# A split-product attention and MoE kernel on one core: the second chunk in whole float32 products with its softmax sums from ones beside the values, and each weight conversion issued behind a named ScalarE instruction

## The chip, the cores and the metric

The kernel runs on one core of one Trainium2 chip. The metric is device time in microseconds of one execution, taken as the median of several; lower is better. The core has TensorE (PE, matrix products), VectorE (DVE), ScalarE (ACT), GpSimd (POOL) and SyncE (SP, which issues the transfers here). In the profile PEld is TensorE loading the operand that stays in place, and a line number such as L460 is the line of the kernel as listed below.

## The reference, cut to what matters

```python
def _attn_ref(q, k, v, n_sink, window):          # B, H, S, D = 4, 8, 768, 64; n_sink, window = 4, 128
    scores = scale * np.matmul(q, k.transpose(0, 1, 3, 2))
    keep = is_sink | in_window                   # the first n_sink keys, and the last `window` keys up to the query
    scores = np.where(keep, scores, -1000000000.0)
    scores = scores - np.max(scores, axis=-1, keepdims=True)
    a = np.exp(scores)
    a = a / (np.sum(a, axis=-1, keepdims=True) + 1e-09)
    return np.matmul(a, v)

def _moe_ref(x, w_in, w_out, s, b):              # x: 3072 x 512, w_in: 512 x 2048, w_out: 2048 x 512
    h = x @ w_in
    r = np.maximum(h, 0.0)
    g = s * (r * r) + b
    return g @ w_out
```

The heads' outputs, put side by side, are the rows of `x`. All inputs and the result are float32.

## The kernel before, in words

The 3072 rows are cut into eight chunks of 384 queries: chunk c is half c % 2 of batch c // 2. For each chunk there is an attention part, which produces `x` (transposed: 512 features in four blocks `cc` of 128 partitions, 384 columns), and an MoE part over 16 blocks f of 128 of the 2048 hidden units.

**Split products.** Most products are made from operands split into a high part in float32r (a rounded form that TensorE takes in one pass) and a low part, the rest. A product is then hi*hi + hi*lo + lo*hi, or fewer where one operand holds both. The MoE works so: `l1(f)` makes twelve products of 384 columns (L521), then ScalarE takes the relu out of PSUM (L524), VectorE squares and scales (L525), ScalarE adds b and rounds to the high part (L527), VectorE makes the low part (L528). `l2(f)`, two blocks later, makes nine products of 512 columns into three PSUM banks `po` (L539).

**Attention, split form** (`attn_slots`, chunks 1 to 7). A unit is (head, block of 128 queries): 24 a chunk. `prep_head` splits the queries (L268 on ScalarE, L272 on VectorE), keys (L271, L273 on GpSimd) and values (L277, L278 on GpSimd). `unit_a` makes scores (L293, L294), VectorE takes minimum and mask in one custom instruction (L298), ScalarE the exponential with its sum (L304), GpSimd copies the 16 columns of the sinks aside (L305). `unit_b`, two slots later, transposes (L316, L317), ScalarE and VectorE split the result (L321, L322); at the end of a pair of heads the sums become reciprocals of 128x6 (L327 to L331). `unit_c` multiplies with the values (L354) and adds the two halves (L362, L363); `unit_d` adds the sinks' part and multiplies by the reciprocals, spread by a product (L378, L380 to L384).

**Chunk 0, whole form** (`first_slots`). Here there is nothing yet to overlap with, and its 384 keys hold the sinks too, so it works in plain float32 products, which TensorE does in several passes: scores (L443), masked minimum (L445), exponential with its sum (L449). `fn` turns the sums of a head into reciprocals of 128x3 (L457, L458) and multiplies the exponentials by them (L460), before `fb` transposes them (L468) and ScalarE copies them out (L472); `fc` multiplies with the values (L480), and the result is split into `x` (L482 on ScalarE, L483 on VectorE).

**Weights.** A block of weights arrives as 64-bit floating-point numbers and is converted on the chip in half steps `make_weight(j)`: two ScalarE operations (L198, L199), two of VectorE (L200, L201) and one of GpSimd (L203) rebuild a float32; then ScalarE rounds the high part (L208) and VectorE, for every fourth block GpSimd, makes the low part (L214). Block f's raw numbers lie in block f+1's place. The first eight places are in a pool of their own, the rest in the pool `late`, which takes the memory of the pool `first` when chunk 0 is done. `weights(n_load, n_make)` calls for so many loads and half steps. By the end of chunk 0's slots four half steps have been called for; within the first MoE chunk, `before(f)` calls for 2f + 5.

**Order.** The MoE of one chunk and the attention of the next are traced in turns, one MoE step and about one attention slot at a time. The framework then orders each engine's instructions by that order as a priority and by when its planner thinks operands and buffers are ready, so an instruction can be put ahead of earlier ones on its engine. Each engine executes its own queue in order. Chunks go 0, 1, 2, ..., 7, and the last MoE chunk has no attention beside it.

Of the kernel before, what the change touches and what calls it, by code (L numbers as in the profile page):

```python
# [33 lines left out]
E0, LB0, LC0 = 8, 4, 6  # L34
# [4 lines left out]
def tile_kernel(ctx, tc, qT, kT, k0, v, vsk, n_sink, window, w, s, b, out):  # L39
# [15 lines left out]
    m_all = first.tile([P, 6 * P], MDT, tag="m", name="m_all")  # L55
# [360 lines left out]
    def first_slots():  # L416
        k = Chunk()

        q = [wk.tile([P, NCC, CH], F32, tag=f"x{i}", name=f"q0{i}") for i in range(2)]
        k.x = [wk.tile([P, NCC, CH], F32R, tag=f"x{i}", name=f"x{i}_0") for i in range(2)]  # L420
        kk = first.tile([P, NCC, CH], F32, tag="k0", name="k0")
        vv = first.tile([P, NCC, CH], F32, tag="v0", name="v0")
        cc, tt, zz, sms = {}, {}, {}, {}

        def load():
            nc.gpsimd.memset(q[0][D:], 0.0)
            nc.vector.memset(q[1][:D], 0.0)
            for ps_ in (slice(0, 1), slice(1, NCC)):
                for hh in range(2):
                    hs = slice(hh * D, (hh + 1) * D)  # L430
                    nc.sync.dma_start(q[hh][hs, ps_, :], qT[0, ps_, hs, :CH].rearrange("r e s -> e r s"))
                    if hh == 0:
# [4 lines left out]
        def fa(h, i):
            pr = h // 2
            n = (i + 1) * P
            u = h * BLK + i  # L440
            uu = slice(u, u + 1)
            sc = psO.tile([P, 512], F32, tag="po", name="sc0")
            nc.tensor.matmul(sc[:, :n], q[h % 2][:, pr, i * P:(i + 1) * P], kk[:, pr, :n], start=True, stop=True)  # L443
            sm = first.tile([P, CH], F32, name="sm0", tag="sm0", bufs=E0)
            nc.vector.tensor_tensor_reduce(out=sm[:, :n], in0=sc[:, :n], in1=m_full[i], scale=-0.125, scalar=BIG,  # L445
                                           op0=ALU.add, op1=ALU.min, accum_out=negm[:, uu])
            if i == 0:
                zz[h] = first.tile([P, 2, BLK], F32, name="z0", tag="z0", bufs=4)
            nc.scalar.activation(sm[:, :n], sm[:, :n], AF.Exp, bias=negm[:, uu], scale=-1.0, accum_out=zz[h][:, 0, i:i + 1])  # L449
# [38 lines left out]
        def slot(t):  # L488
            def f():
# [255 lines left out]
```

## Time and profile before

| what | value |
|---|---|
| median of three runs | 781.66 us (780.46 to 782.41) |
| the profiled execution, its own time | 781.77 us |
| its span, first to last instruction | 780.0 us |
| TensorE busy | 735.3 us, 94% of the span |
| weight loads of TensorE | 656.9 us, 84% |
| VectorE, ScalarE, GpSimd busy | 513.6, 495.5, 268.8 us |
| mean granted TensorE clock | 0.981 |
| moved by transfers | 54.21 MB, mean 70 GB/s |

The times of one instruction in a group are means; matmuls overlap one another, so 1536 of them at 343 ns are busy for only 299.5 us. A row of the groups gives engine, operation, what it writes and reads, its count, its busy time and mean, and then how long its engine sat idle just before it and what ended that. Records on VectorE and ScalarE overlap the next one by some tens of nanoseconds.

### The profile page before, as it was taken

Reading aid. Unit: us, or ns where it says so; the run is one execution under the profiler, and the core shown is the slowest. Engines: PE = TensorE matmul, PEld = TensorE weight load, DVE = VectorE, ACT = ScalarE, POOL = GpSimd, SP = SyncE. Lnnn points to the kernel's source line nnn. Section 1 sums busy time; section 2 is a strip of 40 time slices with the busy share of each in tenths; the row PEclk is TensorE's granted clock in tenths of the full one; section 3 lists DMA queues with packets and bytes.
Section 4 is the critical chain, followed back from the end, with each engine's and each line's share of the span. In section 5 each row is a group of like instructions: output and inputs, shape, how many; then the busy total and the mean of one; then the engine's idle time right before and its main releaser. Section 6 shows DMA issues by size and latency. Waiting matters only on the chain.

```text
span 780.0 us, 12112 instructions
## 1 busy us (share of the span) xinstructions
PE 735.3 (94%) x4036; PEld 656.9 (84%) x4036; DVE 513.6 (66%) x1250; ACT 495.5 (64%) x1231; POOL 268.8 (34%) x411
## 2 busy tenths in 40 slices
PE   7977988699999999999999999999999999999996
PEld 4655776579999999899999999899989999899985
DVE  6879998985676467655676466665676466663231
ACT  4886977766666576656666576656666576643222
POOL 3057668652343233322243233332343233210000
PEclk9989999999999999999999999999999999999998
DMA  7636205212112212112112212112111212001001
GB/s 271 273 103 229 105 14 170 76 34 77 42 54 59 73 43 67 35 43 76 43 53 57 76 43 62 40 43 76 43 53 55 77 43 60 21 1 42 1 1 45
DMA packets 28118, 54.21 MB, mean 70 GB/s; under 512 B 3600, under 2 KB 16528, under 8 KB 26128
## 3 DMA queue, kind: packets, MB, share of 16 engines
q1 hardware_dynamic: 28048, 53.36, 21.3%
q8 instruction: 34, 0.56, 0.3%
q14 instruction: 36, 0.29, 0.1%
HBM read 47.06 MB, written 6.29 MB: 68 GB/s over the span
## 4 chain that ended last, share of the span: by engine, by line
PE 76%; DVE 8%; ACT 7%; issue 3%; POOL 3%; DMA 2%; SPq 1%; ACTq 0%; POOLq 0%; DVEq 0%
PE h L521 30%; PE po L539 30%; PE o L354 5%; PE sc L294 2%; PE sc L293 2%; PE tp L317 2%; PE tp L316 2%; ACT w L199 1%; DVE r L525 1%; DMA w<-in_w 1%; PE o L480 1%; POOL w L203 1%; DVE w L201 1%; DVE qs L272 1%; ACT sm L304 1%
## 5 line engine op out<-in xcount | busy, mean ns | idle before, releaser
L521 PE MATMUL h<-x,w 128*128 128x384 f32 x1536 | 299.5, 343 | 8.7 <-DVE hl L322 3.8
L539 PE MATMUL po<-w,g 128*128 128x512 f32 x1152 | 301.6, 403 | 5.7 <-ACT g L527 3.7
L521 PEld LDWEIGHTS h<-x,w 128*128 128x128 f32 x1536 | 269.7, 190 | 14.5 <-issue 4.0
L539 PEld LDWEIGHTS po<-w,g 128*128 128x128 f32 x1152 | 211.6, 191 | 47.7 <-ACT g L527 4.9
L524 ACT ACTIVATE r<-h 128x384 f32<-128x384 f32 x128 | 62.9, 491 | 103.9 <-PE h L521 96.9
L298 DVE CUSTOM_DVE_ANT_0 sm<-sc,msk 128x272 f32<-128x272 f32 (+1 forms) x168 | 70.2, 418 | 78.4 <-PE sc L294 55.9
L525 DVE SCALAR_TENSOR_TENSOR r<-r,sb 128x384 f32<-128x384 f32 x128 | 84.1, 657 | 54.1 <-ACT r L524 54.0
L528 DVE SCALAR_TENSOR_TENSOR g<-r,sb,g 128x384 fp32r<-128x384 f32 x128 | 85.5, 668 | 45.6 <-ACT g L527 43.5
L305 POOL COPY psk<-sm 128x48 f32<-128x48 f32 x168 | 52.2, 311 | 162.9 <-ACT sm L304 161.7
L304 ACT ACTIVATE sm<-sm,negm 128x272 f32<-128x272 f32 (+1 forms) x168 | 85.4, 508 | 23.3 <-DVE negm L298 22.3
L527 ACT ACTIVATE g<-r,sb 128x384 fp32r<-128x384 f32 x128 | 78.7, 614 | 33.2 <-DVE r L525 32.1
L273 POOL TENSOR_TENSOR kl<-kraw,kh 128x544 fp32r<-128x544 f32 (+1 forms) x56 | 74.9, 1337 | 56.8 <-ACT kh L271 55.5
L321 ACT CAST hl<-tp 128x256 fp32r<-128x256 f32 (+1 forms) x168 | 58.8, 352 | 26.4 <-PE tp L317 26.2
L354 PE MATMUL o<-hl,vv 128*128 128x256 f32 (+1 forms) x400 | 71.4, 295 | 1.1 <-DVE hl L322 0.8
L322 DVE TENSOR_TENSOR hl<-tp,hl 128x256 fp32r<-128x256 f32 (+1 forms) x168 | 66.8, 398 | 7.5 <-ACT hl L321 6.7
L278 POOL TENSOR_TENSOR vv<-vraw,vv 128x256 fp32r<-128x256 f32 (+1 forms) x56 | 41.9, 747 | 60.9 <-ACT vv L277 59.0
L354 PEld LDWEIGHTS o<-hl,vv 128*128 128x128 f32 x400 | 54.9, 190 | 2.7 <-DVE hl L322 1.1
L293 PE MATMUL sc<-kh,qs 128*128 128x272 f32 (+1 forms) x168 | 47.8, 284 | 5.8 <-DVE hl L322 4.7
L363 DVE TENSOR_TENSOR xm<-o,y 64x384 f32<-64x384 f32 x56 | 31.0, 553 | 31.5 <-ACT y L362 31.3
L294 PE MATMUL sc<-kl,qs 128*128 128x272 f32 (+1 forms) x168 | 48.5, 289 | 0.0
L203 POOL TENSOR_TENSOR w<-w 128x1024 int32<-128x1024 int32 (+1 forms) x17 | 32.6, 1921 | 42.4 <-DVE z L458 19.3
L317 PE MATMUL tp<-identr,sm 128*128 128x128 f32 x168 | 45.7, 272 | 0.0
(112 smaller groups left out, 852.0 us busy)
## 6 DMA issues: line engine op xcount, KB each, us to landing
w<-in_w SPq DMA_DIRECT2D x15, 1024.0 KB, 8.9
kraw<-in_kT SPq DMA_DIRECT2D x32, 272.0 KB, 2.7
out<-ot SPq DMA_DIRECT2D x24, 256.0 KB, 2.0
qraw<-in_qT SPq DMA_DIRECT2D x28, 192.0 KB, 2.4
kraw<-in_kT SPq DMA_DIRECT2D x24, 208.0 KB, 2.4
vraw<-in_v SPq DMA_DIRECT2D x16, 256.0 KB, 2.7
vraw<-in_v SPq DMA_DIRECT2D x12, 192.0 KB, 2.3
vsraw<-in_vsk SPq DMA_DIRECT2D x28, 64.0 KB, 1.8
```

Of the source, the lines that this page charges most:

```text
L273: nc.gpsimd.tensor_tensor(out=hd.kl[:, :kw], in0=hd.k[:, :kw], in1=hd.kh[:, :kw].bitcast(F32), op=ALU.subtract)
L293: nc.tensor.matmul(sc[:, :n], hd.qs[:, qs], hd.kh[:, c0:c0 + n], start=True, stop=False)
L294: nc.tensor.matmul(sc[:, :n], hd.qs[:, qs], hd.kl[:, c0:c0 + n], start=False, stop=True)
L298: nc.vector.tensor_tensor_reduce(out=sm[:, :n], in0=sc[:, :n], in1=m, scale=-0.125, scalar=BIG, op0=ALU.add, op1=ALU.min, accum_out=negm[: ...
L304: nc.scalar.activation(sm[:, :n], sm[:, :n], AF.Exp, bias=negm[:, uu], scale=-1.0, accum_out=pp.zz[:, i, hh:hh + 1])
L322: nc.vector.tensor_tensor(out=lo, in0=tp[:, a:z], in1=hi.bitcast(F32), op=ALU.subtract)
L354: nc.tensor.matmul(hd.o[:, q0:q0 + n * P], hd.vv[:, kb, :], hd.hl[:, t, c0 * P:(c0 + n) * P], start=(hd.n == 0), stop=(i == BLK - 1 and kb ...
L521: nc.tensor.matmul(h[:, :CH], weight[f][:, 0, wi, cc * P:(cc + 1) * P], x[xi][:, cc, :], start=(i == 0), stop=(i == 11))
L525: nc.vector.scalar_tensor_tensor(out=r, in0=r, scalar=s_ap, in1=r, op0=ALU.mult, op1=ALU.mult)
L527: nc.scalar.activation(gg[:, 0, :], r, AF.Identity, bias=b_ap, scale=1.0)
L528: nc.vector.scalar_tensor_tensor(out=gg[:, 1, :], in0=r, scalar=b_ap, in1=gg[:, 0, :].bitcast(F32), op0=ALU.add, op1=ALU.subtract)
L539: nc.tensor.matmul(po[tb], gg[:, gi, tsl], weight[f][:, 1, wi, :], start=(f == 0 and i == 0), stop=(f == NF - 1 and i == 2))
```

## The change

1. `first_slots` becomes `plain_slots(c)`, used for chunk 0 and for the second chunk processed. The order of the chunks becomes 0, 2, 1, 3, 4, 5, 6, 7, so that the second one is again a first half, whose 384 keys hold the sinks.
2. In the whole form the normalization moves: `fn` and the exponential's sum are gone. Beside a head's 64 value columns stand 64 columns of ones, so the product with the values (unchanged in its count of columns) gives the values' sum on 64 partitions and the exponentials' sum on the other 64. `fc` then adds 1e-9, takes the reciprocal and multiplies, each on 64 partitions by 384 columns on VectorE; ScalarE rounds `x` for a pair of heads and GpSimd makes its low part.
3. The values of both chunks are loaded in pieces of 64 numbers, one transfer for each pair and half. Queries of the second chunk are loaded per head into tiles whose other half GpSimd sets to zero.
4. Each half step of conversion is issued, on ScalarE, behind the newest exponential of chunk 0 or relu of the first MoE chunk (`gate[-1]`). Half steps are called for earlier: one for every second slot from slot 9 on (nine by the end of chunk 0), then 2f + 11 in `before(f)`.
5. The lags within chunk 0 shrink by one slot each (LB0 3, LC0 5), and the mask tile moves to another pool.

```diff
-E0, LB0, LC0 = 8, 4, 6
+E0, LB0, LC0 = 8, 3, 5
+ORDER = 0, 2, 1, 3, 4, 5, 6, 7
...
-    def first_slots():
+    def plain_slots(c):
...
+                for pr in range(rs.start, rs.stop):
+                    for hh in range(2):
+                        hs = slice(hh * D, (hh + 1) * D)
+                        nc.sync.dma_start(v0[:, pr, :, hh, hs], v[0, pr, :, :BLK, hh, :])
...
+        def load_pair(pr):
+            kt = wk.tile([P, 544], F32, tag="kh", name="k_p")
+            nc.sync.dma_start(kt[:, :CH], k0[bb, :, pr, :])
+            for hh in range(2):
...
+                q[h] = wk.tile([P, CH], F32, tag="qs", name="q_p")
+                nc.gpsimd.memset(q[h][other], 0.0)
+                nc.sync.dma_start(q[h][own], qT[bb, pr, own, :CH])
+                vv[h] = wk.tile([P, 4, P], F32, tag="vv", name="v_p", bufs=VB)
+                nc.gpsimd.memset(vv[h][:, :BLK, other], 1.0)
+                nc.sync.dma_start(vv[h][:, :BLK, own], v[bb, pr, :, :BLK, hh, :])
...
-            nc.scalar.activation(sm[:, :n], sm[:, :n], AF.Exp, bias=negm[:, uu], scale=-1.0, accum_out=zz[h][:, 0, i:i + 1])
+            e = nc.scalar.activation(sm[:, :n], sm[:, :n], AF.Exp, bias=negm[:, uu], scale=-1.0)
+            if c == 0:
+                gate.append(e)
...
-        def fn(h, i):
...
-            nc.vector.tensor_scalar(out=sm[:, :n], in0=sm[:, :n], scalar1=z[:, 0, i:i + 1], scalar2=None, op0=ALU.mult)
...
-            nc.scalar.copy(k.x[0][hs, pr, :], o[hs, :CH])
-            nc.vector.tensor_tensor(out=k.x[1][hs, pr, :], in0=o[hs, :CH], in1=k.x[0][hs, pr, :].bitcast(F32), op=ALU.subtract)
+            if h % 2 == 0:
+                xs[pr] = wk.tile([P, CH], F32, tag="xm", name="xm_p")
+            y = wk.tile([P, CH], F32, tag="y", name="y_p", bufs=1)
+            nc.vector.tensor_scalar(out=y[own], in0=o[other, :CH], scalar1=1e-9, scalar2=None, op0=ALU.add)
+            nc.vector.reciprocal(out=y[own], in_=y[own])
+            nc.vector.tensor_tensor(out=xs[pr][own], in0=o[own, :CH], in1=y[own], op=ALU.mult)
+            if h % 2 == 1:
+                x = xs.pop(pr)
+                nc.scalar.copy(k.x[0][:, pr, :], x)
+                nc.gpsimd.tensor_tensor(out=k.x[1][:, pr, :], in0=x, in1=k.x[0][:, pr, :].bitcast(F32), op=ALU.subtract)
...
+        lb, lc = (LB0, LC0) if c == 0 else (2, 4)
+        ahead = {max(2 * BLK * pr - 3, 0): pr for pr in range(H // 2)} if c else {}
...
-            nc.scalar.activation(r, h[:, :CH], AF.Relu, scale=1.0 / WUP)
+            e = nc.scalar.activation(r, h[:, :CH], AF.Relu, scale=1.0 / WUP)
+            if before:
+                gate.append(e)
...
-            make_weight(made[0])
+
+            with tc.issue_after(gate[-1].ins):
+                make_weight(made[0])
...
-        weights(f + 2 + LOADS // 2, 2 * f + 5)
+        weights(f + 3 + LOADS // 2, max(2 * f + 11, 0))
...
-        if i >= 22 and i % 2 == 0:
-            weights(NEARLY - 1, (i - 20) // 2)
+        if i >= 9:
+            weights(NEARLY - 1, (i - 9) // 2)
...
-            k, slots = attn_slots(c + 1)
+            k, slots = (plain_slots if j == 0 else attn_slots)(ORDER[j + 1])
```

`tc.issue_after(ins)` makes the ScalarE instructions traced inside it stand behind `ins` in ScalarE's queue; it adds no wait on another engine.

More of the change, by code (lines that the diff above doesn't have):

```diff
@@ L54, in tile_kernel @@
     late = []
-    m_all = first.tile([P, 6 * P], MDT, tag="m", name="m_all")
+    m_all = wk.tile([P, 6 * P], MDT, tag="xsk", name="m_all", bufs=1)
     m_full = [m_all[:, a * P:(a + j + 1) * P] for j, a in ((0, 0), (1, 1), (2, 3))]
@@ L413, in attn_slots, with halves, load_all @@
         return k, [slot(t) for t in range(n + LC + LD)]
-    def first_slots():
+    def plain_slots(c):
         k = Chunk()
[L419 to L428, printed above, removed]
+        k.c, bb = c, c // 2
+        q, kk, vv, cc, tt, xs = {}, {}, {}, {}, {}, {}
+        if c == 0:
+            q0 = [wk.tile([P, NCC, CH], F32, tag=f"x{i}", name=f"q0{i}") for i in range(2)]
+            k0_ = first.tile([P, NCC, CH], F32, tag="k0", name="k0")
+            v0 = first.tile([P, NCC, BLK, 2, P], F32, tag="v0", name="v0")
+            for h in range(H):
+                q[h] = q0[h % 2][:, h // 2, :]
+                kk[h] = k0_[:, h // 2, :]
+                vv[h] = v0[:, h // 2, :, h % 2, :]
+        k.x = [wk.tile([P, NCC, CH], F32R, tag=f"x{i}", name=f"x{i}_{c}") for i in range(2)]
+        def halves(h):
+            own, other = slice(0, D), slice(D, P)
+            return (own, other) if h % 2 == 0 else (other, own)
+        def load_all():
+            nc.gpsimd.memset(q0[0][D:], 0.0)
+            nc.vector.memset(q0[1][:D], 0.0)
+            for rs in (slice(0, 1), slice(1, NCC)):
@@ L445, in fa @@
+            nc.tensor.matmul(sc[:, :n], q[h][:, i * P:(i + 1) * P], kk[h][:, :n], start=True, stop=True)
+            if c == 0:
+                sm = first.tile([P, CH], F32, name="sm0", tag="sm0", bufs=E0)
+            elif i < 2:
+                sm = wk.tile([P, W], F32, name="sm_p", tag="sm", bufs=SMB)
+            else:
+                sm = wk.tile([P, 544], F32, name="sm_p2", tag="kl")
             nc.vector.tensor_tensor_reduce(out=sm[:, :n], in0=sc[:, :n], in1=m_full[i], scale=-0.125, scalar=BIG,
@@ L470, in fb @@
             t0, c0 = i // 2, i % 2 * P
-            out = tt[h][:, t0:t0 + i + 1, c0:c0 + P]
-            nc.scalar.copy(out, tp[:, :(i + 1) * P].rearrange("p (k c) -> p k c", c=P))
+            nc.scalar.copy(tt[h][:, t0:t0 + i + 1, c0:c0 + P], tp[:, :(i + 1) * P].rearrange("p (k c) -> p k c", c=P))
         def fc(h):
-            pr, hs = h // 2, slice(h % 2 * D, (h % 2 + 1) * D)
+            pr = h // 2
+            own, other = halves(h)
             o = ps("o0")
@@ L505, in slot @@
+                if 0 <= t - lc < n and (t - lc) % BLK == BLK - 1:
+                    fc((t - lc) // BLK)
             return f
-        return k, [slot(t) for t in range(n + LC0)]
+        return k, [slot(t) for t in range(n + lc)]
     def moe_steps(x, store, wk, before=None, last=False):
```

73 lines of the change are left out of this document (35 added, 38 removed).

## The prediction, made before the changed kernel ran

> **What bounds the kernel now.** I read the busy times by stretch first, cutting the span where the critical chain shows the first layer-1 group of a new MoE chunk.
>
> ```profile
> 0.00:47.50 47.50, 36.61 (x153) 23.74 (x154) 35.06 (x131) 33.74 (x92) 11.02 (x26) 0.93 0.60 223
> 47.50:177.60 130.10, 106.10 (x523) 88.04 (x522) 119.66 (x197) 101.51 (x204) 87.51 (x77) 0.93 0.32 111
> 177.60:264.05 86.45, 85.97 (x494) 79.22 (x493) 55.60 (x148) 55.86 (x152) 27.99 (x53) 1.00 0.19 55
> 264.05:353.45 89.40, 89.07 (x517) 82.29 (x517) 57.57 (x148) 58.33 (x152) 29.70 (x53) 1.00 0.18 55
> 705.11:780.00 74.89, 67.53 (x338) 60.66 (x337) 19.95 (x33) 20.26 (x37) 0.73 (x1) 0.96 0.07 23
> ```
>
> Columns: stretch, length, busy PE, weight loads, VectorE, ScalarE, GpSimd, granted clock, DMA share, GB/s. From 177.6 to 705.1 TensorE has no gaps: three stretches of 86.45 us (attention of an even chunk beside the MoE) alternate with three of 89.4 (odd), 527.5 together. The last stretch has no attention. The change reaches none of these from inside. All there is to win lies before 177.6: in 47.5:177.6 TensorE idles 24.0 of 130.1 us, and the fullest engine is VectorE, 119.66 of 130.1 (92%). Over both stretches VectorE is busy 154.7 and idle 22.9 us.
>
> I then asked what fills VectorE up to 178, in groups.
>
> ```profile
> L201 DVE SCALAR_TENSOR_TENSOR w<-w,wt 128x1024 int32<-128x1024 int32 (+1 forms) x17 | 19.7, 1165 | 0.1
> L214 DVE TENSOR_TENSOR w<-w,w 128x1024 fp32r<-128x1024 f32 (+1 forms) x14 | 17.2, 1226 | 2.4 <-ACT w L208 2.3
> L528 DVE SCALAR_TENSOR_TENSOR g<-r,sb,g 128x384 fp32r<-128x384 f32 x16 | 16.0, 997 | 1.1 <-ACT g L527 1.1
> L200 DVE TENSOR_SCALAR wt<-w 128x1024 int32<-128x1024 int32 (+1 forms) x17 | 15.6, 923 | 4.9 <-ACT w L199 2.8 <-PE o L480 2.0
> L525 DVE SCALAR_TENSOR_TENSOR r<-r,sb 128x384 f32<-128x384 f32 x16 | 14.5, 903 | 0.0
> L272 DVE TENSOR_TENSOR qs<-qraw,qs 64x384 fp32r<-64x384 f32 x10 | 12.6, 1264 | 0.6 <-ACT qs L268 0.3
> L298 DVE CUSTOM_DVE_ANT_0 sm<-sc,msk 128x272 f32<-128x272 f32 x24 | 10.4, 432 | 0.5 <-PE sc L294 0.3
> L322 DVE TENSOR_TENSOR hl<-tp,hl 128x256 fp32r<-128x256 f32 x24 | 9.9, 414 | 0.1
> L460 DVE TENSOR_SCALAR sm<-sm,z 128x128 f32<-128x128 f32 (+2 forms) x24 | 9.4, 447 | 0.1
> L445 DVE CUSTOM_DVE_ANT_0 sm<-sc,m_all 128x128 f32<-128x128 f32 (+2 forms) x24 | 9.3, 417 | 1.6 <-PE sc L443 1.5
> L483 DVE TENSOR_TENSOR x<-o,x 64x384 fp32r<-64x384 f32 x8 | 4.4, 553 | 0.2
> L363 DVE TENSOR_TENSOR xm<-o,y 64x384 f32<-64x384 f32 x8 | 4.4, 550 | 0.1
> L382 DVE TENSOR_TENSOR xm<-zb,xm 128x384 f32<-128x384 f32 x4 | 2.2, 556 | 0.3
> L381 DVE TENSOR_TENSOR xm<-os,xm 128x384 f32<-128x384 f32 x4 | 2.2, 554 | 1.5 <-PE os L378 1.4
> L370 DVE TENSOR_TENSOR xsk<-ts,xsk 32x384 fp32r<-32x384 f32 x4 | 2.2, 550 | 0.1
> L445 DVE DVE_READ_ACCUMULATOR2_ANT negm<- 128x1 f32 x24 | 2.0, 81 | 0.0
> L298 DVE DVE_READ_ACCUMULATOR2_ANT negm<- 128x1 f32 x24 | 1.9, 80 | 0.0
> ```
>
> The first, second and fourth rows are weight conversion, which no edit shortens; the idle column shows VectorE hardly waiting. So up to 178 the time follows VectorE's work plus what idles.
>
> **Part 1, chunk 0 loses its normalization.** `fn` (L457, L458, L460) and the low part at L483 go.
>
> ```profile
> L457 DVE TENSOR_SCALAR z<-z x8: 150/162/171, 9.8 to 40.7; 128x3 f32<-128x3 f32 x8
> L458 DVE RECIPROCAL z<-z x8: 160/175/178, 10.2 to 41.5; 128x3 f32<-128x3 f32 x8
> L327 DVE TENSOR_SCALAR zr<-zz x28: 156/173/658, 79.8 to 690.7; 128x6 f32<-128x6 f32 x28
> L328 DVE RECIPROCAL zr<-zr x28: 173/190/192, 80.3 to 691.2; 128x6 f32<-128x6 f32 x28
> ```
>
> (Minimum, median, maximum in ns.) Removed from VectorE: 9.4 + 4.4 + 8 x (0.162 + 0.175) = 16.5 us.
>
> **Part 2, the second chunk (now chunk 2) leaves the split products.** Of VectorE go 10.4 + 1.9 (L298), 9.9 (L322), eight of ten at L272 (10.1), 4.4 (L363), 6.6 (L382, L381, L370) and 4 x (0.173 + 0.190) = 1.5 at L327 and L328: 44.8 us (two copies of six columns left out). In come masked minima like chunk 0's: 9.3 + 2.0 = 11.3 us.
>
> **Part 3, sums from ones.** Each head of both chunks gets, on 64x384, an add of 1e-9 from PSUM, a reciprocal and a product: 16 times. Add and product cost L483's 0.553 each. The reciprocal at 384 columns is in no row. If what it exceeds the plain op by were all fixed, it would cost about L483's 0.55 (low end). The line through the medians (175 at 3, 190 at 6) has 5.0 ns an element, so 175 + 381 x 5.0 = 2.08 us; the steepest, from 160 to 192, has 10.7 and gives 4.2 (high end). Nearest to both rows is the excess over the plain op: 10 to 13 ns at 3 elements, 17 at 6, about 3 ns an element on top of the plain rate (L483's 553 ns less some 150 fixed, over 384 elements, is 1.05 ns), so about 4.15 ns an element: 0.15 + 384 x 4.15 = 1.75 us. I take 1.75. The Trainium skill, "VectorE: DVE Perf Modes", section "First, the fixed hardware budget", says that the reciprocal is an iterated divide with a repeat count of 8; at eight cycles of its 0.96 GHz an estimate for 384 elements is 3.2 us, and the sum below would come to about 790. The six-element row does not bear that out: it exceeds the plain op by 17 ns, where seven more cycles for each of six would be 44.
>
> Added by parts 2 and 3: 11.3 + 16 x (2 x 0.553 + 1.75) = 57.0 us; removed 61.3. VectorE's operations shrink by 4.3 us only: the reciprocals (28 us) eat what the splits gave.
>
> **Part 4, GpSimd.** The second chunk drops key and value splits and the copies at L305.
>
> ```profile
> L273 POOL TENSOR_TENSOR kl<-kraw,kh 128x544 fp32r<-128x544 f32 (+1 forms) x10 | 17.5, 1750 | 5.4 <-ACT kh L271 4.0 <-issue 1.3
> L305 POOL COPY psk<-sm 128x48 f32<-128x48 f32 x24 | 13.3, 559 | 4.6 <-ACT sm L304 4.5
> L278 POOL TENSOR_TENSOR vv<-vraw,vv 128x256 fp32r<-128x256 f32 (+1 forms) x10 | 9.1, 908 | 8.7 <-ACT vv L277 8.7
> L525 DVE SCALAR_TENSOR_TENSOR r<-r,sb 128x384 f32<-128x384 f32 x16 | 10.0, 626 | 4.0 <-ACT r L524 4.0
> L528 DVE SCALAR_TENSOR_TENSOR g<-r,sb,g 128x384 fp32r<-128x384 f32 x16 | 9.9, 617 | 5.5 <-ACT g L527 4.9
> ```
>
> Eight of ten at L273 and L278, and L305: 34.6 of 98.5 us. It gains 18 memsets (zeroed query halves, halves of ones) and chunk 0's four low parts; by L278's 0.908 us for 256 columns an estimate is 18 x 0.35 + 4 x 1.4 = 12. The last two rows are the same VectorE lines in 179 to 265: 626 and 617 ns against 903 and 997 before 178, 10.5 us in all, where GpSimd is busy 67% against 32%. With a net quarter to a third of GpSimd gone I give back a third: 4 us (bounds 0 and 10.5). ScalarE, 101.5 of 130.1, loses its operand copies (L268, L271, L277) and keeps an exponential and a copy per unit: it does not become the bound.
>
> **Part 5, TensorE.** One whole float32 product is two instructions; a head's two sets of 768 columns and six transposes cost:
>
> ```profile
> 27.32 1.30 PE o L480 x6
> 28.62 0.33 PE tp L468 x3
> 175.51 2.10 PE po L539 x9
> 177.61 2.10 PE h L521 x12
> ```
>
> Scores 1.30 (as many columns as the values), values 1.30, transposes 0.66: 3.26 a head, 26.1 a chunk. The MoE takes 16 x 4.20 = 67.2 us, so a split chunk takes 19.2 (even) to 22.2 (odd). The second stretch carries 93.3 instead of 89.4; within 130 this is covered, and it is the floor if VectorE gets quick.
>
> **Part 6, order.** The six full stretches now hold chunks 1, 3, 4, 5, 6, 7: four odd, two even. 4 x 89.4 + 2 x 86.45 = 530.5, **+3.0 us**, with no cover.
>
> **Part 7, conversion behind a named ScalarE instruction, starting at slot 9, nine half steps by the end of chunk 0 instead of four.** Now ScalarE stops dead on the first weight's transfer, and VectorE behind it:
>
> ```profile
> 16.70 1.10 ACT L198 ACTIVATE w<-w 128x1024 int32<-128x1024 uint32 x1 [2.94 <-DMA w<-in_w]
> 18.59 0.17 DVE L457 TENSOR_SCALAR z<-z 128x3 f32<-128x3 f32 x1 [3.51 <-ACT sm L449]
> 7.80 5.88 SPq L171 DMA_DIRECT2D w<-in_w  x7
> ```
>
> Held behind a later exponential, the conversion cannot stop it: 3.5 us of VectorE idle go, and with work two weights ahead I let another 2 to 4 of its 22.9 go. Behind the gate on ScalarE stands the next exponential, delayed by one conversion step at most; GpSimd's L203 and the copy L208 wait for the conversion, as before. SP's queue: chunk 0's values come in eight transfers instead of two, six more issues ahead of the weights; at the 0.84 us of the seven weight issues above that is 5 us, landing near 21.7 instead of 16.7. The first half step is due at slot 11, some 2.7 heads after the first head's sums (9.8 in the row of L457), and a head is 1.41 + 2.86 = 4.3 us of VectorE: 21.4. So it is just covered; if not, a microsecond or two.
>
> **The sum.** VectorE up to the mark: 154.7 - 0.9 x (4.3 + 4) = 147.2 (0.9 because records overlap: the groups add up to about 171 where the engine is busy 154.7). Idle 22.9 - 3.5 - 3 = 16.4, less some 1.5 at the end, where conversions finish earlier: 15. The mark moves from 177.6 to 162. Then 530.5, then the 76.7 from 705.1 to the profiled execution's 781.77. **769 us**, against 781.77; the median of the runs is 781.66, so nothing to convert. The likeliest case's own range is 762 to 777 (reciprocal 1.4 to 2.1, relief 0 to 10).
>
> **Rivals.**
> *TensorE becomes the bound.* Reciprocal at the low end: 16 x 1.2 x 0.9 = 17 less, the mark at 145; chunk 0 near 47 and 93.3 at a few per cent idle give 146 anyway. **753.** Against: the reciprocal's excess grows from three elements to six.
> *The reciprocals cost more than the splits did: slower.* Place: VectorE, three-op end of each head. The gain of 12.8 is gone at 1.75 + 12.8 / (16 x 0.9) = 2.64 us each; midway between that and the high end, 3.4, gives 769 + 24 = **793**. For it: extrapolation from six elements to 384, and VectorE's 92%. Against: the excess of 17 ns. (The rule on the repeat count in part 3 would end here.)
> *A wait on SP takes the stall's place: no gain.* Query and value buffers of a pair come free only when the pair before is done, and SP issues in order; it already waits so for the keys:
>
> ```profile
> SPq L250 <- POOL kl L273: 66.7, 8, 15.7
> 50.31 5.05 DMA kraw<-in_kT
> ```
>
> If weights from the eighth on queue behind such waits, three pairs at 5.05 us cost 15, with 3 back from idle: **781**. Against: two buffers per tag where keys had one.
>
> **How the numbers follow.** VectorE-bound gain 0.55; TensorE-bound 0.17; dear reciprocal 0.14; SP wait 0.14. A measurement here tells 0.3%, 2.3 us, from no change. Faster: 0.55 + 0.17 + a third of the SP case = 0.76; within 0.3%: half of the SP case and a little of the dear one, 0.08; slower 0.16. Cases of both signs matter, so the range runs from 752 (just under the TensorE floor) to 788 (inside the dear case): about 0.12 left out.
>
> **What would show it.** Right: a RECIPROCAL row of 64x384 x16 near 1.75 us; no idle of ScalarE on the first weight's transfer; the first group of twelve of the second MoE chunk near 162; later stretches 86.4 and 89.4 in the new order; L525 and L528 nearer 620 ns early on. Wrong: that row above 2.64, a VectorE share near 97% up to a mark past 178, or SP waiting with weights due and TensorE idle behind them.

## The result, and the profile after

The changed kernel takes **794.87 us** (median of four runs, 794.39 to 795.44) against 781.26 us for the kernel before beside it: ratio 1.0173, interval 1.0156 to 1.0191. It is slower by 1.7%, where the prediction had 769 us. Line numbers from here on are those of the kernel a row comes from. In the changed kernel the conversion's VectorE lines are L201, L202 and L215, and the end of a head is L515 (add), L516 (reciprocal), L517 (product), L520 (ScalarE rounds) and L521 (GpSimd's low part).

The busy times of the changed kernel by stretch, cut at the first MoE product, then at the mark, which is counted back from the later chunks (the second MoE chunk's first product starts at 187.0), and then by MoE chunk; columns as in the prediction's first fence:

```profile
0.00:57.30 57.30, 40.96 (x159) 25.47 (x159) 48.05 (x107) 32.80 (x66) 17.54 (x34) 0.88 0.59 197
57.30:188.00 130.70, 106.51 (x488) 88.36 (x488) 115.50 (x152) 78.28 (x138) 61.13 (x42) 0.91 0.26 92
188.00:277.45 89.45, 88.67 (x514) 81.49 (x513) 58.73 (x150) 58.87 (x152) 30.76 (x53) 1.00 0.19 59
277.45:366.90 89.45, 89.13 (x518) 82.31 (x517) 57.66 (x148) 58.20 (x152) 29.94 (x53) 1.00 0.19 55
718.51:793.40 74.89, 67.65 (x339) 60.77 (x337) 19.94 (x33) 20.39 (x37) 0.85 (x1) 0.98 0.06 23
```

From the mark on all went as before: two odd chunks stand next to each other at 89.45 us, and the last stretch has 74.89 us in both kernels. The mark itself is at 188.0 instead of 177.6 us; with the new order that gives the span, 793.4 against 780.0 us. VectorE up to the mark: 163.55 us busy and 24.4 idle, where 154.7 and 22.9 stood before and 147.2 and 15 were forecast. Its groups up to the mark (of the changed kernel):

```profile
L516 DVE RECIPROCAL y_p<-y_p 64x384 f32<-64x384 f32 x16 | 40.7, 2546 | 0.3
L202 DVE SCALAR_TENSOR_TENSOR w<-w,wt 128x1024 int32<-128x1024 int32 (+1 forms) x17 | 18.5, 1093 | 0.1
L569 DVE SCALAR_TENSOR_TENSOR g<-r,sb,g 128x384 fp32r<-128x384 f32 x16 | 15.6, 977 | 0.9 <-ACT g L568 0.7
L566 DVE SCALAR_TENSOR_TENSOR r<-r,sb 128x384 f32<-128x384 f32 x16 | 12.7, 797 | 3.5 <-ACT r L563 3.5
L515 DVE TENSOR_SCALAR y_p<-o 64x384 f32<-64x384 f32 x16 | 8.9, 555 | 5.4 <-PE o L510 4.5 <-ACT sel L139 0.5
L517 DVE TENSOR_TENSOR xm_p<-o,y_p 64x384 f32<-64x384 f32 x15 | 8.3, 553 | 0.3
```

The add and the product cost the 0.55 us they were given; the reciprocal takes 2.55 us and is by far VectorE's largest group. The other large loss is at the end of chunk 0. TensorE's waits for chunk 0's `x` in 40 to 80 us (in the kernel before it has none; its longest wait there follows), and VectorE's queue in that place:

```profile
PE h L560 <- DVE xm_p L517: 7.6, 1, 7.6
PE h L560 <- POOL x L521: 2.1, 1, 2.1
```

```profile
PE tp L468 <- DVE sm L460: 3.5, 1, 3.5
```

```profile
57.55 2.55 DVE L516 RECIPROCAL y_p<-y_p 64x384 f32<-64x384 f32 x1
60.02 1.39 DVE L201 TENSOR_SCALAR wt<-w 128x1024 int32<-128x1024 int32 x1
61.44 0.55 DVE L517 TENSOR_TENSOR xm_p<-o,y_p 64x384 f32<-64x384 f32 x1
61.92 1.21 DVE L202 SCALAR_TENSOR_TENSOR w<-w,wt 128x1024 int32<-128x1024 int32 x1
63.16 0.55 DVE L515 TENSOR_SCALAR y_p<-o 64x384 f32<-64x384 f32 x1
63.74 2.19 DVE L201 TENSOR_SCALAR wt<-w 128x1024 int32<-128x1024 int32 x1
65.96 2.55 DVE L516 RECIPROCAL y_p<-y_p 64x384 f32<-64x384 f32 x1
68.54 1.23 DVE L202 SCALAR_TENSOR_TENSOR w<-w,wt 128x1024 int32<-128x1024 int32 x1
69.80 0.56 DVE L517 TENSOR_TENSOR xm_p<-o,y_p 64x384 f32<-64x384 f32 x1
```

The rows of the last two heads (57.55 and 65.96 are their reciprocals) alternate with conversion pieces (L201, L202), and each piece stands in the one queue ahead of the next step of a head. Chunk 0's products with the values and the low parts of its `x`, in the changed kernel and then in the kernel before (minimum, median, maximum in ns, first and last start in us):

```profile
L510 PE MATMUL o<-tt,v x48: 272/400/1008, 13.2 to 57.2; 128*128 128x384 f32 x16, 128*128 128x256 f32 x16, 128*128 128x128 f32 x16
L521 POOL TENSOR_TENSOR x<-xm_p,x x4: 1009/1302/1978, 24.8 to 71.7; 128x384 fp32r<-128x384 f32 x4
```

```profile
L480 PE MATMUL o<-tt,v x48: 272/421/1006, 14.1 to 49.4; 128*128 128x384 f32 x16, 128*128 128x256 f32 x16, 128*128 128x128 f32 x16
L483 DVE TENSOR_TENSOR x<-o,x x8: 541/555/565, 19.8 to 51.8; 64x384 fp32r<-64x384 f32 x8
```

Before, the last low part of `x` starts 2.4 us after the last product of chunk 0; now it starts 14.5 us after it, and it ends at 73.7 instead of 52.4 us. TensorE has only pieces of the first MoE step, and some scores of the second chunk, until then. So the 10.4 us by which the mark is later are two parts of opposite sign: chunk 0's last low part starts 19.9 us later (71.7, before 51.8), and the stretch from there to the mark is 9.5 us shorter (116.3, before 125.8). The granted clock of TensorE is lower in that place too: 0.68 in 40 to 60 us and 0.73 in 60 to 80 us, before 0.83 and 0.96.

### The profile page after: what moved, and what is told of

The parts are those of the page before. It is cut to its first block, busy times and chain, and to the rows that moved or that the text cites. A ratio compares the mean times of both kernels' runs of the same rounds, so it can differ in the third digit from the quotient of the medians.

```text
span 793.4 us, 11907 instructions
## 1 busy us (share of the span) xinstructions
PE 742.9 (94%) x4024; PEld 661.2 (83%) x4024; DVE 525.9 (66%) x1182; ACT 474.8 (60%) x1139; POOL 252.3 (32%) x385
## 4 chain that ended last, share of the span: by engine, by line
PE 76%; DVE 4%; ACT 2%; POOL 1%; issue 1%; DMA 0%; ACTq 0%; POOLq 0%
PE h L560 31%; PE po L580 29%; PE o L355 5%; PE sc L295 2%; PE sc L294 2%; PE tp L318 2%; PE tp L317 2%; DVE y_p L516 1%; PE o L510 1%; PE ts L368 1%; PE os L379 1%; PE zb L381 1%; POOL w L204 1%; ACT g L568 1%; DVE xsk L371 0%
## 5 line engine op out<-in xcount | busy, mean ns | idle before, releaser
L566 DVE SCALAR_TENSOR_TENSOR r<-r,sb 128x384 f32<-128x384 f32 x128 | 82.1, 642 | 58.2 <-ACT r L563 58.0
L569 DVE SCALAR_TENSOR_TENSOR g<-r,sb,g 128x384 fp32r<-128x384 f32 x128 | 85.2, 666 | 43.8 <-ACT g L568 42.0
L299 DVE CUSTOM_DVE_ANT_0 sm<-sc,msk 128x272 f32<-128x272 f32 (+1 forms) x144 | 61.0, 423 | 76.8 <-PE sc L295 62.2
L568 ACT ACTIVATE g<-r,sb 128x384 fp32r<-128x384 f32 x128 | 78.7, 615 | 28.5 <-DVE r L566 27.2
L306 POOL COPY psk<-sm 128x48 f32<-128x48 f32 x144 | 38.6, 268 | 162.4 <-ACT sm L305 161.4
L305 ACT ACTIVATE sm<-sm,negm 128x272 f32<-128x272 f32 (+1 forms) x144 | 73.7, 511 | 20.8 <-DVE negm L299 20.0
L274 POOL TENSOR_TENSOR kl<-kraw,kh 128x544 fp32r<-128x544 f32 (+1 forms) x48 | 62.4, 1300 | 52.7 <-ACT kh L272 51.9
L322 ACT CAST hl<-tp 128x256 fp32r<-128x256 f32 (+1 forms) x144 | 51.3, 356 | 28.2 <-PE tp L318 27.9
L323 DVE TENSOR_TENSOR hl<-tp,hl 128x256 fp32r<-128x256 f32 (+1 forms) x144 | 57.9, 402 | 8.0 <-ACT hl L322 7.2
L355 PE MATMUL o<-hl,vv 128*128 128x256 f32 (+1 forms) x352 | 61.8, 294 | 0.0
L279 POOL TENSOR_TENSOR vv<-vraw,vv 128x256 fp32r<-128x256 f32 (+1 forms) x48 | 34.6, 720 | 56.3 <-ACT vv L278 53.9
L516 DVE RECIPROCAL y_p<-y_p 64x384 f32<-64x384 f32 x16 | 40.7, 2546 | 0.3
L294 PE MATMUL sc<-kh,qs 128*128 128x272 f32 (+1 forms) x144 | 40.5, 282 | 0.0
```

The lines of the kernel that those rows point to most:

```text
L274: nc.gpsimd.tensor_tensor(out=hd.kl[:, :kw], in0=hd.k[:, :kw], in1=hd.kh[:, :kw].bitcast(F32), op=ALU.subtract)
L323: nc.vector.tensor_tensor(out=lo, in0=tp[:, a:z], in1=hi.bitcast(F32), op=ALU.subtract)
L355: nc.tensor.matmul(hd.o[:, q0:q0 + n * P], hd.vv[:, kb, :], hd.hl[:, t, c0 * P:(c0 + n) * P], start=(hd.n == 0), stop=(i == BLK - 1 and kb ...
L566: nc.vector.scalar_tensor_tensor(out=r, in0=r, scalar=s_ap, in1=r, op0=ALU.mult, op1=ALU.mult)
L568: nc.scalar.activation(gg[:, 0, :], r, AF.Identity, bias=b_ap, scale=1.0)
L569: nc.vector.scalar_tensor_tensor(out=gg[:, 1, :], in0=r, scalar=b_ap, in1=gg[:, 0, :].bitcast(F32), op0=ALU.add, op1=ALU.subtract)
```

## The experiments

Each median stands beside runs of the kernel before on the same chip (781.5 to 781.8 us in all groups, which is why medians of different groups are set beside each other below); the interval is of the ratio to it. "Old schedule" is the kernel before's: four half steps by the end of chunk 0, 2f + 5 in `before(f)`, no gate.

**1. The reciprocals.** Their work taken away (the attention is then not normalized), or halved.

```diff
-            nc.vector.reciprocal(out=y[own], in_=y[own])
+            nc.vector.tensor_tensor(out=y[own], in0=y[own], in1=y[own], op=ALU.mult)
```

> The changed kernel with each of the 16 reciprocals of 64x384 replaced by a product of the same shape (the outputs are therefore not normalized rightly; everything else is as changed). Theory A (VectorE's work up to the second MoE chunk sets the time, and the reciprocal at 2.55 us is the term that was mis-sized): 16 x (2.55 - 0.55) = 32 us of VectorE less, 0.9 of it on the path, so 766 us, with the mark of the second MoE chunk near 159 instead of 188. Theory B (the loss is the earlier conversions, which stand in VectorE's queue ahead of chunk 0's last heads): at most half of that, 780 or more. Theory C (whole float32 products keep TensorE back): about 790.

```diff
+            nc.scalar.copy(xs[pr][own], o[own, :CH])
             if h % 2 == 1:
+                nc.vector.reciprocal(out=y, in_=y)
+                nc.vector.tensor_tensor(out=x, in0=x, in1=y, op=ALU.mult)
```

> The changed kernel with one reciprocal and one product for each pair of heads, on 128 partitions by 384, and the sums' numerators copied out of PSUM by ScalarE. Theory A, if a reciprocal's time goes by its columns and not by its partitions: 8 x (2.55 + 0.55) = 25 us of VectorE less, 0.9 of it on the path, 773 us. If it goes by elements in all, 128 partitions would take 5 us and nothing but the products is saved: 790. Theory B: 787 or more.

Measured: 779.48 us (0.9964 to 0.9991) without them, 779.54 us (0.9972 to 0.9991) with one for a pair. Both take some 15.4 us off. The rows (first kernel, then second):

```profile
L516 DVE TENSOR_TENSOR y_p<-y_p 64x384 f32<-64x384 f32 x16 | 15.2, 951 | 0.4
```

```profile
L520 DVE RECIPROCAL y_p<-y_p 128x384 f32<-128x384 f32 x8 | 20.4, 2548 | 0.1
```

So VectorE's records fell by 25.5 and, by the reciprocals alone, 20.3 us, for 15.4 us of time. That is less than theory A's 0.9 of it, whose times (766 and 773 us) were 13 and 6 us too low. The version with pairs also has eight products fewer on VectorE and sixteen copies more on ScalarE. And 128 partitions cost what 64 do, so the pair's form is half price.

**2. The conversion schedule.** Old schedule in the changed kernel, new schedule with the gate in the kernel before, and the gate alone (old counts) in the kernel before.

```diff
-            with tc.issue_after(gate[-1].ins):
-                make_weight(made[0])
+            make_weight(made[0])
...
-        weights(f + 3 + LOADS // 2, max(2 * f + 11, 0))
+        weights(f + 2 + LOADS // 2, 2 * f + 5)
...
-        if i >= 9:
-            weights(NEARLY - 1, (i - 9) // 2)
+        if i >= 22 and i % 2 == 0:
+            weights(NEARLY - 1, (i - 20) // 2)
```

> The changed kernel with the conversion schedule of before: no gate, four half steps by the end of chunk 0, 2f + 5 afterwards. Theory A: the same VectorE work has to be done before the mark in any order, so 795 within 3 us. Theory B: chunk 0's x is ready some 8 to 10 us sooner and the time falls to 785 to 788.

> The kernel before with only the new conversion schedule: the gate, nine half steps by the end of chunk 0, 2f + 11 afterwards. Theory A: no VectorE work is added, so 781 within 3 us, or up to 3.5 us faster because ScalarE no longer stops on the first weight. Theory B: slower by 5 to 10 us, 786 to 791, since conversions again stand ahead of chunk 0's last heads.

> The kernel before with only the gate: each conversion's ScalarE instructions behind the newest exponential or relu traced before it, the counts of half steps as before. Theory A: same work, and ScalarE no longer stops on the first weight, 778 to 781. Rival: without the gate the planner had already pulled conversions forward into chunk 0's idle times; held back, three weights fewer are ready at the first MoE step, and the time grows by 6 us or more, 788 and up.

Measured: 791.24 us (1.0114 to 1.0148) for the changed kernel with the old schedule, so the new one costs it 3.6 us; 788.31 us (1.0075 to 1.0109) for the kernel before with the new one, 6.7 us slower; 781.45 us (0.9988 to 1.0008) with the gate alone. The schedule that was to fill idle time loses time by itself, and it is the counts that lose it, not the gate at the old counts.

**3. The order alone**, in the kernel before.

```diff
+    ORDER = 0, 2, 1, 3, 4, 5, 6, 7
```

> The kernel before with only the order of chunks changed to 0, 2, 1, 3, 4, 5, 6, 7, all but chunk 0 in split form. The six full stretches gain 3.0 us (four odd and two even instead of three and three). The second stretch has an even chunk, whose VectorE work is some 2 us less, and it is bound by VectorE: 781.6 + 3 - 2 = 782.6. If the second stretch did not care which chunk it has, 784.6.

Measured: 784.18 us (1.002 to 1.0045), 2.7 us more.

**4. No wide reciprocals at all, and hardly any VectorE work in their place.** Both whole chunks are normalized as chunk 0 was before, with small reciprocals, but the exponentials are multiplied on ScalarE; once with the new schedule, once with the old.

```diff
+            nc.scalar.activation(sm[:, :n], sm[:, :n], AF.Identity, scale=z[:, 0, i:i + 1])
```

> The changed kernel with the normalization of before's chunk 0 (a reciprocal of 128x3 a head, each exponential multiplied before it is transposed) in both whole-form chunks, the multiplication on ScalarE. VectorE loses 3.65 us a head and gets 0.9 back: 16 x 2.77 = 44 us of records, about 40 of busy time. In the first four experiments about 0.7 of VectorE's busy time came out of the total (22.5 us less busy gave 16.5 us less time where the reciprocal was replaced by a product). Theory A therefore gives 795 - 28 = 767. Rival: ScalarE, which takes 48 more instructions of some 0.5 us, becomes the bound, and the gain stops near 780.

> As the run before it, with the conversion schedule of before and no gate. If the schedule costs by itself what the second and third experiment showed (3.6 us with the long reciprocals, 6.7 us on the kernel before), 761 to 764. If it only cost because VectorE was full, the same as the run before it, 767.

Measured: 794.20 us (1.0151 to 1.0184) with the new schedule, 780.06 us (0.997 to 0.9989) with the old. This was the run that broke the theory that VectorE's work sets the time: up to the mark VectorE is busy 125.2 of 186.4 us in the first and 124.2 of 171.3 in the second (columns as before).

```profile
0.00:186.40 186.40, 147.44 (x630) 111.77 (x631) 125.16 (x258) 136.25 (x303) 61.40 (x68) 0.88 0.37 124
0.00:171.30 171.30, 139.76 (x630) 106.47 (x631) 124.15 (x258) 135.59 (x303) 61.27 (x68) 0.94 0.40 135
```

Same work, 14 us apart, by nothing but when weights are loaded and converted. ScalarE, the rival of the expectation, has the same work in both as well. Of the 15.1 us between the marks 7.7 are TensorE's own busy time, for the same 630 products, at a granted clock of 0.88 instead of 0.94; the rest is idle. So a part of the difference shows as longer products. The clock is lower in the run where TensorE idles more (39.0 us, the other 31.5); what lowers it was not tested.

**5. Which half of the schedule.** The version of 4 with only the half steps inside chunk 0 early, with only those of the first MoE chunk early (both with the gate), and with the new counts but no gate.

> The version with the normalization on ScalarE and the gate, with the half steps of conversion early inside chunk 0 (nine by its end), but 2f + 5 in the first MoE chunk. Between 780.1 (old schedule) and 794.2 us (new). Theory that the half steps inside chunk 0 stand ahead of its last heads and delay x: 790 to 794, last x of chunk 0 near 63 us. Theory that the pile of half steps at the first MoE steps costs: 780 to 783, last x near 53.

> The complement: four half steps by the end of chunk 0 and 2f + 11 from the first MoE step on, with the gate. Theory of the half steps inside chunk 0: 780 to 783 us. Theory of the pile at the first MoE steps: 788 to 794 us. If both pay a part: 785 to 788 in both runs.

> The version with the normalization on ScalarE and the new counts, each half step free to be placed by the framework instead of behind a named ScalarE instruction. If only the counts matter: 794 us. If the gate holds the ScalarE parts late and so the VectorE parts in front of later heads: 780 to 788 us.

Measured: 784.86 us (1.0023 to 1.0061), 790.46 us (1.01 to 1.0151) and 789.98 us (1.0076 to 1.0124). Against 780.06 that is 4.8 us for the early slots and 10.4 for 2f + 11; together 15.2, measured 14.1. At these counts the gate adds 4.2 us (794.20 less 789.98). Both halves pay, the MoE steps the larger part, and neither theory holds by itself. With the early slots chunk 0's last low part does start late, as the first theory said: at 62.9 us, with the old schedule at 51.2, with 2f + 11 alone at 52.6. But the time grows by only 4.8 us in the median (8.6 in that profiled execution), so a part of these 11.7 comes back later. TensorE's waits show both halves. In 44 to 95 us, with 2f + 11 alone:

```profile
PE po L586 <- ACT g L574: 13.7, 3, 6.3
```

and with the old schedule:

```profile
PE po L586 <- DVE g L575: 2.7, 2, 1.7
PE po L586 <- ACT g L574: 0.9, 2, 0.5
```

VectorE's queue in that place with 2f + 11 (L201, L202, L215 are conversion, L572 the first MoE step's square):

```profile
57.65 1.22 DVE L215 TENSOR_TENSOR w<-w,w 128x1024 fp32r<-128x1024 f32 x1
58.78 2.38 DVE L201 TENSOR_SCALAR wt<-w 128x1024 int32<-128x1024 int32 x1
61.09 0.41 DVE L481 CUSTOM_DVE_ANT_0 sm_p<-sc,m_all 128x256 f32<-128x256 f32 x1
61.43 0.08 DVE L481 DVE_READ_ACCUMULATOR2_ANT negm<- 128x1 f32 x1
61.43 1.22 DVE L202 SCALAR_TENSOR_TENSOR w<-w,wt 128x1024 int32<-128x1024 int32 x1
62.57 2.89 DVE L201 TENSOR_SCALAR wt<-w 128x1024 int32<-128x1024 int32 x1
65.38 2.24 DVE L572 SCALAR_TENSOR_TENSOR r<-r,sb 128x384 f32<-128x384 f32 x1
```

The square starts at 65.38 us; with the old schedule the same one starts at 55.15. Seven half steps are due at the first MoE step (11 less 4) and are traced ahead of it. In chunk 0 (20 to 66 us) the wait is another: with the early slots TensorE's transposes wait 9.7 us for ScalarE's product with the sums, where conversion pieces stand between; with the old schedule 4.6.

```profile
PE tp L509 <- ACT sm L497: 9.7, 4, 3.8
```

```profile
PE tp L509 <- ACT sm L497: 4.6, 3, 4.0
```

**6. Other combinations with the old schedule**: paired reciprocals, none, and the helper's normalization on VectorE in both chunks.

> The changed kernel with one reciprocal of 128x384 for each pair of heads and the conversions on the schedule of the kernel before. If the reciprocals (11.7 us) and the schedule (3.6 us) each cost what they cost alone: 791.2 - 15.4 + 0 = about 776 us. If the new schedule only costs where VectorE's queue is full, the version with paired reciprocals has already lost that cost: about 779.5 us, no change to the paired version. If the early conversions fill holes that the shorter VectorE work opens, undoing them loses: 782 us or more.

> The reciprocals replaced by products of the same tile (the attention isn't normalized in either chunk), with the conversions on the schedule of the kernel before. Additive: 779.5 - 3.6 = about 776 us. If the schedule hid part of the gain, as it hid 14 us of it where the normalization left VectorE: 765 to 770 us. If the order of the heads and TensorE's length are the bound by then: 779 us.

> The changed kernel, whole second chunk in float32 products, but normalized by the helper of the kernel before (small reciprocals) in both chunks, and the conversions on the schedule of before. It keeps the 45 us of split-chunk instructions removed and pays the helper in two chunks (16.5 us more for the second). Theory that VectorE's work up to the mark and the schedule set the time: VectorE's raw work 154.7 - 44.8 + 11.3 + 16 = 137 us, so below the paired version: about 770 to 776 us. Theory that TensorE's float32 products (26 us for each whole chunk) and the idle at the start are the bound by then: 779 to 782 us.

Measured: 777.57 us (0.993 to 0.997), 777.08 us (0.9923 to 0.996) and 776.30 us (0.9918 to 0.9957). The first two are 2.0 and 2.4 us under the same with the new schedule, within 1.7 us of additive. The third keeps chunk 0's normalization as it was and has no wide reciprocal at all; it is some 5 us under the kernel before, so the whole second chunk gains with the helper too.

**7. One chunk at a time**, old schedule: the first chunk alone in the new form, then the second alone.

```diff
-            k, slots = (plain_slots if j == 0 else attn_slots)(ORDER[j + 1])
+            k, slots = attn_slots(ORDER[j + 1])
```

> Only the first chunk takes sums from ones beside the values and wide reciprocals; the second chunk stays split, with the heads in the order of before and the conversions on the schedule of before. VectorE gains eight reciprocals of 2.55 us and eight products and loses the helper: 20.4 + 8 x 0.55 + ... - 16.5, about +10 us of raw work. If all of it shows at the mark: 791 us. If chunk 0's place at the start hides half of it: 786 us. If only the second chunk's reciprocals are dear (they stand last): 782 us.

```diff
+            if c == 0:
+                nc.scalar.copy(k.x[0][own, pr, :], o[own, :CH])
+                nc.vector.tensor_tensor(out=k.x[1][own, pr, :], in0=o[own, :CH], in1=k.x[0][own, pr, :].bitcast(F32), op=ALU.subtract)
+                return
...
+                if c == 0 and t % BLK == BLK - 1 and t < n:
+                    for i in range(BLK):
+                        fn(t // BLK, i)
```

> Chunk 0 as in the kernel before (sums with the exponential, normalization by the helper), the second chunk whole with sums from ones and eight wide reciprocals, order 0, 2, 1, old conversion schedule. If the two chunks' costs add (791.2 for both, 796.9 for the first alone): 781.6 + (791.2 - 796.9) = 776 us. If the reciprocals cost wherever they stand, eight of 2.55 us and their adds and products against the helper's instructions, as in the version with the helper in both chunks (776.3): 785 to 789 us.

Measured: **796.90 us** (1.0174 to 1.0223) for the first alone, **768.56 us** (0.9814 to 0.9882) for the second alone. The two parts of the change have opposite signs. The second chunk alone is 1.5% faster than the kernel before, although its eight reciprocals are as dear as in the changed kernel and its order costs 2.7. It came out 7 us under the lower of its two forecasts; the first alone 6 us over the highest of its three. With the helper in the second chunk, in experiment 6, it was 776.30 us: there the sums from ones are 7.7 us better than the helper, with 10 us more VectorE work up to the mark (148.3 us, with the helper 138.1). The second chunk's lags differ too between these two (2 and 4, with the helper 3 and 5).

Not all of the 13 us come from the second chunk's form. In the profiled executions 6.3 us lie in chunk 0, whose last low part starts at 45.5 us (before 51.8, with the order alone 51.3), and 10.2 us in the stretch from there to the mark (115.6 us, before 125.8); the order takes 3.0 back. Chunk 0's steps are those of the kernel before, but its values come in eight transfers and its mask lies in another pool, and ScalarE does not wait for the first weight's transfer (2.9 us before). Which of these made it earlier was not run alone.

**8. Whose reciprocals.** Those of chunk 0 replaced by products, those of the second chunk kept (both chunks in the new form); and the second chunk alone with a reciprocal for each pair.

```diff
+            if c == 0:
+                nc.vector.tensor_tensor(out=y[own], in0=y[own], in1=y[own], op=ALU.mult)
+            else:
+                nc.vector.reciprocal(out=y[own], in_=y[own])
```

> Both chunks with sums from ones, old conversion schedule (791.2 us), the eight reciprocals of chunk 0 replaced by products of the same tile (chunk 0's attention isn't normalized), those of the second chunk kept. With all sixteen replaced it gave 777.1. If chunk 0's alone cost the time: 777 to 779 us. If the sixteen cost alike: 784 us. If the second chunk's cost it: 790 us.

> Chunk 0 as in the kernel before, the second chunk with sums from ones and one reciprocal of 128x384 for each pair of heads: four fewer than in the version that gave 768.6 us, 10 us of VectorE work. If the second chunk's reciprocals are covered by TensorE's work: the same within 2 us. If VectorE's work still sets the time: 759 to 764 us.

Measured: 780.00 us (0.9975 to 0.9994) and 773.23 us (0.9879 to 0.9912). Chunk 0's eight cost 11.2 us (791.24 to 780.00), the second chunk's at most 2.9 more (to 777.08), and halving those in the faster version won nothing. That version came out 4.7 us slower. Its chunk 0 has the same code, but in its trace TensorE's clock in 10 to 20 us is 0.66 where the version with eight has 1.00, and its last low part of `x` starts at 50.3 instead of 45.5 us:

```profile
10.00:20.00 10.00, 7.28 (x25) 5.48 (x25) 5.65 (x31) 4.72 (x18) 0.79 (x4) 0.66 0.85 221
```

```profile
10.00:20.00 10.00, 8.00 (x42) 5.88 (x42) 8.36 (x45) 7.92 (x31) 0.78 (x4) 1.00 0.97 251
```

(Pairs first, then eight.) That execution was 3.9 us above the version's median and had the lowest mean clock of its five (0.981, the other four 0.988 to 0.991; the version with eight has 0.987 to 0.991). So the clock in this trace does not account for the 4.7 us between the medians, and what does stays open. A difference of some 4 us between two versions is therefore no evidence of a cause by itself.

What the reciprocals do to chunk 0 is seen with both chunks in the new form and the old schedule (experiment 2): busy times up to the mark, and the low parts of chunk 0's `x`.

```profile
0.00:184.10 184.10, 148.82 (x644) 114.41 (x645) 165.31 (x258) 111.25 (x202) 76.62 (x76) 0.88 0.37 126
L521 POOL TENSOR_TENSOR x<-xm_p,x x4: 1001/1474/1541, 28.2 to 70.0; 128x384 fp32r<-128x384 f32 x4
```

The last low part starts at 70.0 us, and with products in chunk 0 at 53.5 (below). So it is late with the old schedule as well, and conversion pieces stand between a head's steps there too. TensorE's busy time is 7.8 us longer than with the products, at a granted clock of 0.88 instead of 0.96.

What the new form of chunk 0 costs beyond its reciprocals is seen by setting the kernel with products in chunk 0 beside the second chunk alone (779.66 and 768.24 us in the profiled executions). Busy times up to their marks, and the low parts of chunk 0's `x` (products first, helper second):

```profile
0.00:172.40 172.40, 141.07 (x647) 107.98 (x648) 151.79 (x258) 110.63 (x202) 78.86 (x76) 0.96 0.40 136
L524 POOL TENSOR_TENSOR x<-xm_p,x x4: 997/1192/2135, 26.3 to 53.5; 128x384 fp32r<-128x384 f32 x4
```

```profile
0.00:161.10 161.10, 133.91 (x632) 105.11 (x633) 148.27 (x281) 113.49 (x228) 69.91 (x71) 0.97 0.42 143
L528 DVE TENSOR_TENSOR x<-o,x x8: 537/554/561, 18.8 to 45.5; 64x384 fp32r<-64x384 f32 x8
```

The mark is 11.3 us later for 3.5 us more VectorE work, the last low part 8.0 us. The last products of chunk 0 start nearly together, at 44.6 and 43.8 us, but the last low part starts 8.9 us after them in the one and 1.7 in the other: add, product, product, rounding and GpSimd's part follow each other, through a single `y` tile, in a queue with conversions. The helper does its share ahead of the transposes, and leaves one step on VectorE behind the last product. The lags (3 and 5, against 4 and 6) differ between the two as well and were not tried alone.

So the medians lead from the kernel before to the changed one in four steps: 781.7, the second chunk whole **-13** to 768.6, the new form of chunk 0 with products in its reciprocals' place **+11** to 780.0, chunk 0's reciprocals instead of the products **+11** to 791.2, the new schedule **+4** to 794.9. The sizes hold for this sequence; added first, chunk 0's form costs 15, not 23. The last step is no larger than what stayed open above; that the schedule costs rests on the 14.1 us of experiment 4 and the 6.7 us of experiment 2.

The two profiles agree with that. From the second chunk alone to the changed kernel the mark goes from 161.1 to 188.0, 26.9 us later, and chunk 0's last low part from 45.5 to 71.7, 26.2 us later. The stretch between the two is as long in both (115.6 and 116.3 us): nearly all that the rest of the change costs lies ahead of chunk 0's end.

## Why the prediction was wrong

It forecast 769 us, said faster at 0.76, and the range ended at 788. The mark came 26 us late. In its own terms that is 163.55 - 147.2 = 16.3 us of VectorE work and 24.4 - 15 = 9.4 us of idle; part 3 and part 4 below account for 13.3 of the 16.3, and the other 3 were not traced to a group.

- **Part 3, the reciprocal.** This is the term that was mis-sized: 1.75 us taken, 2.546 measured, 16 x 0.796 x 0.9 = 11.5 of the 16.3 us. The reading of the excess over a plain op at three and six elements was the wrong choice between the bounds: the slope from six elements to 384 is (2546 - 190) / 378 = 6.2 ns an element, close to the line through the medians (5.0) that I had set aside. The Trainium skill, "VectorE: DVE Perf Modes", section "First, the fixed hardware budget", gives the repeat count of 8 that I weighed down by the six-element row; the estimate of 3.2 us worked out from it was 0.65 too long, mine 0.8 too short, and the row measures about six cycles of its 0.96 GHz an element.
- **That alone does not reverse the sign.** 2.546 is below the 2.64 at which the rival of the dear reciprocal would decide; with the right price the sum would have been 769 + 11.5 = 780.5, no change. The rival had place and direction right, and its 793 was near, by a price (3.4) that is too high. What it left out is next.
- **The sum's rule, "the time follows VectorE's work plus what idles",** is the step that failed. It let work be removed from one chunk and added to another at the same price, and took idle time for something that only part 7 changes. Chunk 0's end is on the path: until its `x` is whole no MoE step can be finished, and the second chunk did not fill TensorE alone. Work there shows as TensorE waiting (7.6 and 2.1 us above), and most of it shows in the time; eight reciprocals cost 11.2 us in chunk 0 and at most 2.9 in the second. The rule fails the other way too. For the second chunk alone, with the measured reciprocal, it gives 0.9 x (44.8 - 11.3 - 8 x (2 x 0.553 + 2.546)) = 3.9 us off the mark and 3.0 us more behind it, hardly a gain (part 4 left aside); 13 us were measured, and the larger part of the 16.5 by which the mark is earlier is VectorE's idle time, 12.8 us up to the mark instead of 22.9. Part 3 priced the three ops as busy time and never asked what stands behind them in the queue.
- **Part 7, the schedule.** The stall on the first weight's transfer is gone, as said: no engine but SP waits on a weight's transfer up to the mark, where ScalarE waits 5.8 us for them with the old schedule (experiment 2). But the 3.5 + 3 + 1.5 us of idle that it should win did not come. Issued early, a piece of conversion stands ahead of chunk 0's last heads and of the first MoE steps; idle rose to 24.4 us. I costed only what the gate puts ahead of one exponential, not what nine half steps in chunk 0, and two more at each MoE step, put ahead of everything else. Whether an early or a gated conversion helps the version with only the second chunk whole was not run.
- **Part 2** had its rows right: the masked minima of the second chunk came in as forecast (9.5 us in the changed kernel, 9.3 forecast, and their reads). The 13 us of the second chunk alone are not its sum, though, as said above. **Part 5** held: TensorE did not become the bound in any version (the earliest mark, 161.1, has 133.9 us of it).
- **Part 4** was too large: L566 and L569 came to 797 and 977 ns from 903 and 997, 16 x (0.106 + 0.020) = 2.0 us, 2 short (1.8 by the sum's factor of 0.9), though GpSimd's work fell by 98.5 - 78.7 = 19.8 us, near the 22.6 forecast.
- **Part 6** was right: 3.0 forecast, 2.7 measured alone.
- **The rival of the wait on SP** did not show: SP waits, but no engine waited on a transfer behind it once the first keys were there, except one of 2.5 us.

The second chunk alone measures 768.6, near the forecast for the whole change, but by other terms: it keeps the helper in chunk 0 and has no new schedule. That nearness is luck.

## What to carry to other kernels

Price added work by where it stands, not by the engine's total: ask, for each stage's last result, what chain of steps now leads to it and what else is in those queues; eight dear instructions in a stage where TensorE had other work cost at most 2.9 us here, and the same eight at the end of a stage that nothing covers cost 11.2. Work that is called for early is not free either when queues are in order (here it cost 2 to 14 us in every version that was run with both schedules), so a schedule is tested apart from the rest. And when a change has two halves, run each alone: here one gave 1.5% and the other took 2%.

## What the runs showed of the hardware

- VectorE's reciprocal costs by columns: 175 ns for 128x3, 190 for 128x6, 2546 for 64x384 and 2548 for 128x384. So it belongs on all 128 partitions, or on few columns.
- A product of two operands in SBUF, 64x384, took 951 ns in the mean up to the mark (experiment 1), where the same shape with one operand in PSUM took 553 (L517). MoE's square, both operands in SBUF, took 605 to 2246 ns up to the mark in experiment 5 (2f + 11 alone), and the neighbour is GpSimd:

```profile
64.87 2.33 POOL L204 TENSOR_TENSOR w<-w 128x1024 int32<-128x1024 int32 x1
72.64 0.60 DVE L572 SCALAR_TENSOR_TENSOR r<-r,sb 128x384 f32<-128x384 f32 x1
79.77 2.75 POOL L204 TENSOR_TENSOR w<-w 128x1024 int32<-128x1024 int32 x1 [2.50 <-DVE w L202]
80.69 2.25 DVE L572 SCALAR_TENSOR_TENSOR r<-r,sb 128x384 f32<-128x384 f32 x1
```

The square at 65.38 us (2.24 us, above) and the one at 80.69 start while GpSimd is in an instruction and end 0.42 us after it does (67.62 and 67.20, 82.94 and 82.52); the one at 72.64, with GpSimd idle, takes 0.60. So here the long ones lasted as long as GpSimd's instruction did, and their length says little of their own work.
